# Two grouped-query attention blocks on one core: V loaded from GpSimd's DMA queue, and the remainder tiles of P of steps 24 to 125 all transposed by DMA

## The chip, the core and the metric

The kernel runs on one core of a Trainium2 chip. The core has a matrix engine (TensorE, "PE" in the profile), a vector engine (VectorE, "DVE"), a scalar engine (ScalarE, "ACT"), GpSimd ("POOL") and SyncE ("SP"), which here only issues DMAs. Sixteen DMA engines move the data. The metric is device time in microseconds, so lower is better.

## The reference

Two independent problems, A and B, of one shape; their outputs stand side by side.

```python
B, Sq, D = 16, 80, 576
Hq, Hkv, Sk, Dh = 32, 16, 512, 128           # two query heads for each K/V head
q = (x @ wq).reshape(B, Sq, Hq, Dh).transpose(0, 2, 1, 3)
k = jnp.repeat(k_cache, 2, axis=1)           # k_cache, v_cache: [16, 16, 512, 128]
v = jnp.repeat(v_cache, 2, axis=1)
scores = jnp.einsum("bhqd,bhkd->bhqk", q, k) * (Dh ** -0.5)
p = softmax(scores, axis=-1)
o = jnp.einsum("bhqk,bhkd->bhqd", p, v)
out = o.transpose(0, 2, 1, 3).reshape(B, Sq, Hq * Dh) @ wo     # [16, 80, 576]
```

All inputs and outputs are bf16.

## The kernel before, in words

**Steps.** The work is cut into 128 batch steps U. A step is one batch entry and four K/V heads, which is eight query heads, in one of the two problems. Steps 0 to 63 belong to A, 64 to 127 to B. For each step the kernel loads K (512 KB) with one transposing DMA from SyncE's queue (`ldk`, line 612) into one of five `kT` buffers, and V (512 KB) with one plain DMA from SyncE's queue (`ldv`, line 616) into one of four `v_sb` buffers.

**Five tiles of scores.** One K/V head serves two query heads of 80 rows, which makes 160 rows, and a tile has 128. So a step has four full tiles (k = 1 to 4, one for each K/V head) and one remainder tile (k = 0), which gathers the 32 rows left over from each of the four heads. TensorE computes the scores of the full tiles at line 658 (`qk`) and those of the remainder tiles at line 644 (`qkr`). For every tile VectorE takes the row maximum (line 667), ScalarE the exponential with the row sum (line 671), VectorE the reciprocal of the sums (line 677, `rcp`) and GpSimd multiplies P by it (line 680, `nrm`).

**Transposing P.** The product with V needs P with the keys on the partitions. A tile of P is 128x512, so four 128x128 transposes. The usual way is on TensorE, against an identity matrix, into PSUM (line 686, `tr`), and a copy by VectorE into `pT` (line 694 for full tiles, line 692 for the remainder tile; the operation is called `ptev`). For some steps the remainder tile goes another way: one transposing DMA from SyncE's queue writes the same place in `pT` (line 698, `rtr`). Before the change these are the odd steps from 24 to 125 except 50 to 61, 45 steps in all. In such a step the reciprocal is taken in two parts, for tile 0 alone and for tiles 1 to 4 (`RG[1]`), so there is one more reciprocal. `pT` has three buffers. The product with V is line 731 (`pv`), its result is cast into `oT` by ScalarE (line 747).

**The rest.** The projections `x @ wq` (line 540, `qp`) and `o @ wo` (line 781, `op`) are spread between the steps. Their weights come over SyncE's queue too (only problem A's first piece of wq comes from ScalarE's), and so does the output (line 815).

**Order.** Nothing is ordered at run time. A planner (`_Sched.arrange`) simulates the engines and the DMA with durations and costs that are written in the source, picks at each moment the ready operation with the lowest key on each engine, and so writes the order of each engine's instructions; waits on semaphores are put in where data cross engines. Each engine runs its list strictly in order. The planner's numbers for the operations at hand: `nrm` 0.674 us on GpSimd, `ldk` 3.4 us of SyncE, `ldv` 0.45 us of SyncE, `rtr` 1.2 us of SyncE; as DMA cost `KC` for K, `VC` for V and `RDC` (0.78) for `rtr`.

Of the kernel before, what the change touches and what calls it, by code (L numbers as in the profile page):

```python
# [19 lines left out]
NS = 16  # L20
QL0 = 15.0
QL1 = 10.0
KC = 2.95
VK = 8.0
KK = 8.0
DLAT = 1.6
XC = 0.4
QL2 = 10.0
VC = 1.65
WQC = 3.2  # L30
NQ = 3
NWS = 4
# [4 lines left out]
NWC = 4  # L37
BANKS = dict(S=(0, 1, 2, 6), T=(3, 4), O=(5, 7), M=(7, 5), M0=(7, 5, 6, 3, 4), M1=(7, 6), ML=(7, 5, 6, 0, 1))
NML = 12
XDMA = True  # L40
RG = (((0, 1, 2, 3, 4),), ((0,), (1, 2, 3, 4)))
RDMA = (24, 126)
RPER = (1, 3)
RSKIP = ((50, 62),)
XK = (15.0, 15.0)
WQK = 4.0
WQKB = 4.0
# [11 lines left out]
XLD = ((-100.0, -60.0), (-25.0, -24.9))  # L59
XH = -2.0  # L60
WQ1 = -16.8
OPX = ((12.0, 1.8), (18.5, 1.45), (18.5, 1.45), (18.5, 1.45))
LP0 = 18.5
LPS = 1.15
# [29 lines left out]
class _Sched:  # L94
# [40 lines left out]
    def arrange(self):  # L135
# [32 lines left out]
        free = dict((e, 0.9) for e in by_eng)  # L168
        mode = 0
        bank_free = dict((b, 0.0) for b in range(8))  # L170
        dma_free = 1.4
        left = len(ops)
        hold = dict(pe=0.05, dve=0.02, act=0.02, pool=0.0, sp=0.0)

# [30 lines left out]
        while left:  # L205
            best = None
            for e in free:
                cand = []
                for n in by_eng[e]:
                    if at[n] < len(streams[n]):  # L210
                        o = streams[n][at[n]]
                        r = ready(o, free[e])
                        if r is not None:
                            cand.append((r, o))
                if cand:
                    st = max(free[e], min(c[0] for c in cand))
                    if best is None or st < best[0]:
                        best = (st, e, cand)
            assert best is not None, [(streams[n][at[n]].name, [d.name for d in streams[n][at[n]].pre if d.done is None],
                                       len(streams[n][at[n]].alloc)) for n in streams if at[n] < len(streams[n])]  # L220
            now, e, cand = best
            k_, s_, r, o = min(((o.pri, o.seq, r, o) for r, o in cand if r <= now + hold[e]), key=lambda x: x[:2])
            st = max(now, r)
            o.eng = e
            dur = o.dur[e] if isinstance(o.dur, dict) else o.dur
            if e == "pe":
                if o.mode and mode == 0 or o.mode != mode:
                    st = max(st, now + 0.1)
                mode = o.mode
            if o.alloc:  # L230
                for vb, (_, b) in zip(o.alloc, pick(o.alloc, max(r, now))):
                    vb.phys = b
                    bank_free[b] = None
            o.start = st
            free[e] = st + dur
            if o.dsem is not None:
                d0 = max(st + 0.5, dma_free)
                dma_free = d0 + o.cost
                o.done = dma_free + DLAT
            else:  # L240
                o.done = st + dur + o.lat
            for res, ver in o.reads:
                if isinstance(res, _VB):
                    res.left -= 1
                    if res.left == 0:
                        bank_free[res.phys] = o.done
            at[o.stream] += 1
            left -= 1
# [75 lines left out]
def bass_concat_heads__gqa_block_cached__gqa_block_cached__near_ridge_kernel(  # L324
# [27 lines left out]
    with ExitStack() as es:  # L352
# [29 lines left out]
        S = _Sched()  # L382
# [112 lines left out]
        for goct in range(NG):  # L495
# [7 lines left out]
            for pi, (c0, c1) in enumerate(pieces):  # L503
                t_ld = 5.0 * (u0 - lead[goct]) - (WQKB if goct == NG // 2 else WQK)
                if goct < 2:
                    t_ld = (-90.0, WQ1)[goct] + (10.0, 0.02)[goct] * pi
                fr = (c1 - c0) / 1024.0
                dsem = "d_wqs" if goct == 0 and pi == 0 else "d_wqt" if goct == 1 and pi == 0 else "d_wq%d" % wsl
                eng = "act" if goct == 0 else "sp"
                strm = "wqa" if goct == 0 else "wq"  # L510

                def em_ldwa(e, wq_ap=wq_ap, q=q, wsl=wsl, c0=c0, c1=c1):
                    src = wq_ap[0:512, q * 1024 + c0:q * 1024 + c1]
                    return e.dma_start(wq_sb[:, wsl, 0:4, c0:c1], src.rearrange("(c p) n -> p c n", p=128))

                def em_ldwb(e, wq_ap=wq_ap, q=q, wsl=wsl, c0=c0, c1=c1):
                    return e.dma_start(wq_sb[64:128, wsl, 4, c0:c1],
                                       wq_ap[512:576, q * 1024 + c0:q * 1024 + c1])
# [84 lines left out]
        for U in range(NSU):  # L603
# [8 lines left out]
                return e.dma_start_transpose(kT[:, ks, :, :], src)  # L612

            def em_ldv(e, vc_ap=vc_ap, b=b, q=q, vs=vs):
                src = vc_ap[b, 4 * q:4 * q + 4, :, :].rearrange("g (p j) d -> p g (j d)", j=4)
                return e.dma_start(v_sb[:, vs, :, :], src)

            S.add("sp", 5.0 * gfirst[U] + 0.5 * (U - gfirst[U]) - LA - KK, em_ldk, writes=[R(("kT", ks), U)],
                  dsem="d_k%d" % ks, name="ldk%d" % U, stream="K", dur=3.4, cost=KC)
            S.add("sp", 5.0 * U - VK, em_ldv, writes=[R(("V", vs), U)],  # L620
                  dsem="d_v%d" % vs, name="ldv%d" % U, stream="V", dur=0.45, cost=VC)

            vo = None
            rdma = RDMA[0] <= U < RDMA[1] and U % 4 in RPER and not any(a_ <= U < b_ for a_, b_ in RSKIP)
            for k in range(5):
                T = 5 * U + k
                Q = Qof[(U, k)]
# [128 lines left out]
        for prob in range(2):  # L756
            for hh in range(NPAIR):
                for half in range(NPP):
                    for n in range(NB_):
# [47 lines left out]
                        else:  # L807
# [4 lines left out]
                            def em_st(e, rb=rb, c3=c3, prob=prob, slot=slot):  # L812
# [4 lines left out]
                            S.add("dve", xe, em_eb, reads=[R(vb, 0), R(("acc", rb, c3), (prob, hh - 1))],  # L817
                                  writes=[R(("osb", slot), (prob, half, n))], name="oeb%d.%d.%d" % (prob, half, n),
                                  stream="oeb", dur=0.38, ahead=OVO)
                            S.add("sp", xe + 0.3, em_st, reads=[R(("osb", slot), (prob, half, n))],  # L820
                                  dsem="d_out%d" % slot, name="st%d.%d.%d" % (prob, half, n), stream="st",
                                  dur=0.45, cost=0.3)

# [5 lines left out]
        def run_engine(e, name):  # L829
            for op in ops:  # L830
                if op.eng != name:
                    continue
                for ck, v in op.waits:
                    e.wait_ge(sem_of(ck), v)
                inst = op.emit(e, name) if len(op.engs) > 1 else op.emit(e)
                if op.signals:
                    if op.dsem is not None:
                        inst.then_inc(sems[op.dsem], 16)
                    else:
                        inst.then_inc(sems["e_" + name], 1)  # L840
            if name == "sp":
                for i in range(NOSB):
                    n = "d_out%d" % i
                    tot = S.totals.get(("d", n), 0)
                    if tot:
                        e.wait_ge(sems[n], tot)
# [48 lines left out]
```

## Time and profile before

| | us |
|---|---|
| median of 3 runs | 780.52 (779.81 to 781.06) |
| the profiled execution | 780.9 |
| its span, from first to last instruction | 779.2 |
| TensorE busy | 772.0 (99%), granted clock 1.00 |
| VectorE busy | 678.6 (87%) |
| ScalarE busy | 611.6 (78%) |
| GpSimd busy | 432.4 (55%) |
| moved by DMA | 166.44 MB, mean 214 GB/s |

The span is what the trace covers; 1.7 us of the execution's own time lie around it. A busy time of TensorE counts modelled ends of pipelined matmuls, so the share is read together with the time between the starts of instructions. An instruction that issues a DMA counts as no engine's busy time; SyncE's own instructions are seen in the timeline as "SPq".

### The profile page before, as it was taken

The page shows a single profiled execution, that of the slowest core. Times are in us where ns is not written, and L with a number is a line of the kernel's source. Part 1 is how long each engine was busy: PE and PEld are TensorE (multiplying, and loading weights), DVE is VectorE, ACT ScalarE, POOL GpSimd, SP SyncE. Part 2 cuts the span into 40 slices and gives each one's busy share as a digit, 9 for nine tenths or more (in the row PEclk, how much of TensorE's full clock was granted, in tenths as well). Part 3 has the DMA queues.
Part 4 walks back from the last instruction along what each step waited for, and adds up shares of the span by engine and source line. Part 5 has one row for each costly group of instructions (what it writes and reads, how often), then busy time and mean ns, then how long its engine had stood idle before and what let it go on. Part 6 is the DMA issues. An engine that isn't in the chain of part 4 may idle for free.

```text
span 779.2 us, 21256 instructions
## 1 busy us (share of the span) xinstructions
PE 772.0 (99%) x8078; PEld 567.5 (73%) x8078; DVE 678.6 (87%) x1558; ACT 611.6 (78%) x1736; POOL 432.4 (55%) x647
## 2 busy tenths in 40 slices
PE   9999999999999999999999999999999999999998
PEld 5576677777777777767777777777777777777786
DVE  4999988888888899888898899988888888989982
ACT  1878988888888888867787777978888887887860
POOL 1555755565655656555655655655655655664660
PEclk9999999999999999999999999999999999999999
DMA  9999999988899999999999999999999978999951
GB/s 249 226 259 240 249 222 247 203 188 197 205 200 213 204 237 247 251 213 227 211 229 214 177 214 244 258 218 237 221 230 202 200 177 196 257 220 210 187 134 32
DMA packets 386564, 166.44 MB, mean 214 GB/s; under 512 B 300576, under 2 KB 383008, under 8 KB 386464
## 3 DMA queue, kind: packets, MB, share of 16 engines
q1 hardware_dynamic: 385248, 163.91, 95.7%
q8 instruction: 65, 1.06, 0.6%
q10 hardware_dynamic: 1216, 1.18, 0.5%
q14 instruction: 35, 0.29, 0.1%
HBM read 87.46 MB, written 2.95 MB: 116 GB/s over the span
## 4 chain that ended last, share of the span: by engine, by line
PE 91%; DVE 7%; DMA 1%; ACT 0%; POOL 0%; issue 0%; SPq 0%
PE ps L540 20%; PE ps L781 20%; PE ps L731 17%; PE ps L686 15%; PE ps L658 13%; DVE negmax L667 4%; PE ps L644 4%; DVE pT L694 2%; DVE qT L552 1%; DMA kT<-in_A_k_cache_dram 1%; PE ps L409 0%; PE ps L464 0%; DVE pT L692 0%; ACT p_sb L671 0%; PE ps L424 0%; POOL p_sb L680 0%
## 5 line engine op out<-in xcount | busy, mean ns | idle before, releaser
L680 POOL TENSOR_SCALAR p_sb<-p_sb,rinv 128x512 bf16<-128x512 bf16 x640 | 430.0, 692 | 325.5 <-DVE rinv L677 325.1
L671 ACT ACTIVATE p_sb<-ps,negmax 128x512 bf16<-128x512 f32 x640 | 441.3, 693 | 84.0 <-DVE negmax L667 77.1
L667 DVE TENSOR_REDUCE negmax<-ps 128x1 f32<-128x512 f32 x640 | 427.8, 679 | 9.6 <-PE ps L658 5.1
L686 PE MATMUL ps<-ident,p_sb 128*128 128x128 bf16 x2380 | 229.7, 219 | 1.1 <-POOL p_sb L680 0.5
L694 DVE COPY pT<-ps 128x512 bf16<-128x512 bf16 x512 | 209.9, 413 | 16.4 <-PE ps L686 14.2
L731 PE MATMUL ps<-pT,v_sb 128*128 128x160 bf16 x2048 | 222.6, 233 | 0.1
L540 PE MATMUL ps<-xT,wq_sb 128*128 128x480 bf16 (+1 forms) x1280 | 213.2, 300 | 0.1
L731 PEld LDWEIGHTS ps<-pT,v_sb 128*128 128x128 bf16 x2048 | 158.4, 98 | 54.3 <-ACT oT L747 5.9
L686 PEld LDWEIGHTS ps<-ident,p_sb 128*128 128x128 bf16 x2380 | 168.7, 98 | 35.7 <-DVE pT L694 6.5
L658 PE MATMUL ps<-kT,qT 128*128 128x512 bf16 x512 | 189.0, 379 | 0.6 <-ACT p_sb L671 0.6
L781 PE MATMUL ps<-wo_sb,oT 128*128 128x288 bf16 x1280 | 171.5, 286 | 0.0
L540 PEld LDWEIGHTS ps<-xT,wq_sb 128*128 128x128 bf16 x1280 | 106.9, 98 | 61.4 <-ACT oT L747 2.6
L781 PEld LDWEIGHTS ps<-wo_sb,oT 128*128 128x128 bf16 x1280 | 122.8, 98 | 34.8 <-ACT qT L551 1.3
L747 ACT CAST oT<-ps 128x320 bf16<-128x320 f32 x256 | 108.7, 425 | 37.0 <-PE ps L731 36.6
L671 ACT ACTIVATION_READ_ACCUMULATOR p_sb<-ps,negmax 128x1 f32 x640 | 130.1, 203 | 0.0
L551 ACT ACTIVATE qT<-ps 128x160 bf16<-128x160 f32 (+1 forms) x159 | 63.2, 398 | 25.9 <-PE ps L540 24.9
L552 DVE TENSOR_SCALAR qT<-ps 128x480 bf16<-128x480 f32 (+1 forms) x97 | 54.7, 564 | 22.2 <-PE ps L540 21.1
L658 PEld LDWEIGHTS ps<-kT,qT 128*128 128x128 bf16 x512 | 49.2, 98 | 6.3 <-ACT p_sb L671 3.1
L809 DVE TENSOR_TENSOR osb<-ps,acc 128x288 bf16<-128x288 f32 x40 | 18.2, 456 | 27.6 <-PE ps L781 27.4
L644 PE MATMUL ps<-kT,qT 128*32 128x512 bf16 x512 | 39.6, 384 | 1.1 <-DMA kT<-in_A_k_cache_dram 0.9
L677 DVE RECIPROCAL rinv<-rowsum 128x1 f32<-128x1 f32 (+1 forms) x173 | 29.6, 171 | 11.1 <-ACT p_sb L671 11.1
L692 DVE COPY pT<-ps 128x512 bf16<-128x512 bf16 x83 | 34.5, 416 | 4.9 <-PE ps L686 4.7
(19 smaller groups left out, 47.0 us busy)
## 6 DMA issues: line engine op xcount, KB each, us to landing
v_sb<-in_A_v_cache_dram SPq DMA_DIRECT2D x64, 512.0 KB, 4.6
v_sb<-in_B_v_cache_dram SPq DMA_DIRECT2D x64, 512.0 KB, 4.6
wo_sb<-in_A_wo_dram SPq DMA_DIRECT2D x8, 576.0 KB, 7.6
wo_sb<-in_B_wo_dram SPq DMA_DIRECT2D x8, 576.0 KB, 7.4
wq_sb<-in_B_wq_dram SPq DMA_DIRECT2D x4, 1024.0 KB, 6.7
out_dram<-osb SPq DMA_DIRECT2D x40, 72.0 KB, 2.3
wq_sb<-in_A_wq_dram SPq DMA_DIRECT2D x2, 1024.0 KB, 7.4
wq_sb<-in_A_wq_dram ACTq DMA_DIRECT2D x2, 512.0 KB, 6.9
```

Source lines behind the costliest of these rows:

```text
L540: last = e.matmul(ps[:, vb.phys, 0:n1 - n0], lhsT=wq_sb[:, wsl, ck, i * 128:(i + 1) * 128], rhs=xT[:, half, ck, n0:n1], start=(ck == 0), s ...
L551: return e.activation(dst, src, AF.Identity, scale=SCALE)
L644: last = e.matmul(ps[32 * g4:32 * g4 + 32, vb_.phys, :], lhsT=qT[:, qsl_, bl_, g4 * 160 + 128:g4 * 160 + 160], rhs=kT[:, ks_, :, g4 * 128: ...
L658: return e.matmul(ps[:, vb.phys, :], lhsT=qT[:, qsl, bl, gl * 160:gl * 160 + 128], rhs=kT[:, ks, :, gl * 128:(gl + 1) * 128], start=True, ...
L667: return e.tensor_reduce(negmax[:, si:si + 1], ps[:, vb.phys, :], axis=AX.X, op=AluOpType.max, negate=True)
L671: return e.activation(p_sb[:, psl, :], ps[:, vb.phys, :], AF.Exp, bias=negmax[:, si:si + 1], scale=1.0, accum_out=rowsum[:, ss, k:k + 1])
L680: return e.tensor_scalar(p_sb[:, psl, :], p_sb[:, psl, :], rinv[:, ss, k:k + 1], 1.0, op0=AluOpType.mult, op1=AluOpType.mult)
L686: last = e.transpose(psb[:, vt.phys, j * 128:(j + 1) * 128], p_sb[:, psl, j * 128:(j + 1) * 128], ident[:])
L694: return e.tensor_copy(pT[:, pts, :, 0:4, gl * 32:gl * 32 + 32], psb[:, vt.phys, 0:512].rearrange("p (j h c) -> p j h c", j=4, h=4))
L731: last = e.matmul(ps[:, vo.phys, off:off + 160], lhsT=v_sb[:, vs, gl, j * 128:(j + 1) * 128], rhs=pT[:, pts, j, :, gl * 32:gl * 32 + 32], ...
L747: return e.copy(dst, src)
L781: last = e.matmul(ps[:, vb.phys, 0:DC], lhsT=oT[:, hi, rb * 128:(rb + 1) * 128], rhs=wo_sb[:, wi, c3 * DC:(c3 + 1) * DC], start=(hi == 0), ...
```

## The change

V is issued from GpSimd's instruction list instead of SyncE's, one DMA for each step as before, with a planned duration of 1.0 us on GpSimd (`VENG`, `VDUR`, `VN`). The remainder tile of every step from 24 to 125 is transposed by DMA (`RSEL`): 102 steps instead of 45. The planner now keeps one DMA clock for each issuing queue instead of one for all, with a cost of 2.6 for K and 1.8 for V, and writes a new order for all engines with these numbers. The other names (`STENG`, `XSH`, `WQ1B`, `VN`) keep their old meaning at these values.

```diff
-KC = 2.95
+KC = 2.6
-VC = 1.65
+VC = 1.8
...
+VENG = "pool"
+VDUR = 1.0
+VN = 1
+STENG = "sp"
...
-RDMA = (24, 126)
-RPER = (1, 3)
-RSKIP = ((50, 62),)
+RSEL = ((24, 126, (0, 1, 2, 3)),)
...
-        dma_free = 1.4
+        dma_free = {}
...
-                d0 = max(st + 0.5, dma_free)
-                dma_free = d0 + o.cost
-                o.done = dma_free + DLAT
+                d0 = max(st + 0.5, dma_free.get(e, 1.4))
+                dma_free[e] = d0 + o.cost
+                o.done = d0 + o.cost + DLAT
...
-                src = vc_ap[b, 4 * q:4 * q + 4, :, :].rearrange("g (p j) d -> p g (j d)", j=4)
-                return e.dma_start(v_sb[:, vs, :, :], src)
+                src = vc_ap[b:b + VN, 4 * q:4 * q + 4, :, :].rearrange("b g (p j) d -> p b g (j d)", j=4)
+                return e.dma_start(v_sb[:, vs:vs + VN, :, :], src)
...
-            S.add("sp", 5.0 * U - VK, em_ldv, writes=[R(("V", vs), U)],
-                  dsem="d_v%d" % vs, name="ldv%d" % U, stream="V", dur=0.45, cost=VC)
+            if U % VN == 0:
+                S.add(VENG, 5.0 * U - VK, em_ldv, writes=[R(("V", vs + i_), U + i_) for i_ in range(VN)],
+                      dsem="d_v%d" % vs, name="ldv%d" % U, stream="V", dur=VDUR, cost=VN * VC)
...
-            rdma = RDMA[0] <= U < RDMA[1] and U % 4 in RPER and not any(a_ <= U < b_ for a_, b_ in RSKIP)
+            rdma = any(a_ <= U < b_ and U % 4 in m_ for a_, b_, m_ in RSEL)
```

More of the change, by code (lines that the diff above doesn't have):

```diff
@@ L39 @@
 NML = 12
+VENG = "pool"
+VDUR = 1.0
+VN = 1
+STENG = "sp"
+XSH = 0.0
 XDMA = True
 RG = (((0, 1, 2, 3, 4),), ((0,), (1, 2, 3, 4)))
-RDMA = (24, 126)
-RPER = (1, 3)
-RSKIP = ((50, 62),)
+RSEL = ((24, 126, (0, 1, 2, 3)),)
 XK = (15.0, 15.0)
@@ L61 @@
 WQ1 = -16.8
+WQ1B = 0.02
 OPX = ((12.0, 1.8), (18.5, 1.45), (18.5, 1.45), (18.5, 1.45))
@@ L505, in bass_concat_heads__gqa_block_cached__gqa_block_cached__near_ridge_kernel @@
                 if goct < 2:
-                    t_ld = (-90.0, WQ1)[goct] + (10.0, 0.02)[goct] * pi
+                    t_ld = (-90.0, WQ1)[goct] + (10.0, WQ1B)[goct] * pi
                 fr = (c1 - c0) / 1024.0
@@ L819, in bass_concat_heads__gqa_block_cached__gqa_block_cached__near_ridge_kernel @@
                                   stream="oeb", dur=0.38, ahead=OVO)
-                            S.add("sp", xe + 0.3, em_st, reads=[R(("osb", slot), (prob, half, n))],
+                            S.add(STENG, xe + 0.3, em_st, reads=[R(("osb", slot), (prob, half, n))],
                                   dsem="d_out%d" % slot, name="st%d.%d.%d" % (prob, half, n), stream="st",
@@ L840, in run_engine @@
                         inst.then_inc(sems["e_" + name], 1)
-            if name == "sp":
+            if name == STENG:
                 for i in range(NOSB):
```

## The prediction

> **What bounds the kernel now.** I read the engine shares and the chain first, then the groups of L686, L692 and L680.
>
> ```profile
> PE 772.0 (99%) x8078; PEld 567.5 (73%) x8078; DVE 678.6 (87%) x1558; ACT 611.6 (78%) x1736; POOL 432.4 (55%) x647
> ...
> PE 91%; DVE 7%; DMA 1%; ACT 0%; POOL 0%; issue 0%; SPq 0%
> ...
> L680 POOL TENSOR_SCALAR p_sb<-p_sb,rinv 128x512 bf16<-128x512 bf16 x640 | 430.0, 692 | 325.5 <-DVE rinv L677 325.1
> ...
> L686 PE MATMUL ps<-ident,p_sb 128*128 128x128 bf16 x2380 | 229.7, 219 | 1.1 <-POOL p_sb L680 0.5
> ...
> L677 DVE RECIPROCAL rinv<-rowsum 128x1 f32<-128x1 f32 (+1 forms) x173 | 29.6, 171 | 11.1 <-ACT p_sb L671 11.1
> L692 DVE COPY pT<-ps 128x512 bf16<-128x512 bf16 x83 | 34.5, 416 | 4.9 <-PE ps L686 4.7
> ```
>
> TensorE is the path. Its idle time on DMA is about 1 us, on everything else a few us. So a matmul taken away shortens the run, if nothing else is late. The 219 ns of L686 is not the price of a transpose, because matmuls are pipelined; that is read from starts, in the timeline of TensorE:
>
> ```profile
> 305.73 0.39 PE L686 MATMUL ps<-ident,p_sb 128*128 128x128 bf16 x4
> 305.95 0.38 PE L658 MATMUL ps<-kT,qT 128*128 128x512 bf16 x1
> ```
>
> Four transposes hold TensorE for 0.22 us (56 ns each between starts over the whole trace).
>
> Then what is nearly late. SyncE's queue, in the timeline and by stretches (PE, PEld, DVE, ACT, POOL busy; clock; DMA share; GB/s):
>
> ```profile
> 58.39 0.58 SPq L616 DMA_DIRECT2D v_sb<-in_A_v_cache_dram  x1
> 59.02 3.67 SPq L612 DMA_TRANSPOSE kT<-in_A_k_cache_dram  x1
> 62.73 0.58 SPq L616 DMA_DIRECT2D v_sb<-in_A_v_cache_dram  x1
> 63.35 3.64 SPq L612 DMA_TRANSPOSE kT<-in_A_k_cache_dram  x1
> ...
> 7.00:9.00 2.00, 1.81 (x28) 1.60 (x27) 1.15 (x4) 0.19 (x1) 0.00 (x0) 1.00 1.07 374
> 58.00:80.00 22.00, 21.54 (x233) 14.81 (x232) 21.23 (x49) 18.78 (x55) 13.35 (x20) 1.00 1.04 240
> ...
> 300.00:345.00 45.00, 44.04 (x477) 32.61 (x475) 39.86 (x92) 35.98 (x104) 24.96 (x38) 1.00 1.05 247
> ...
> 480.00:540.00 60.00, 60.00 (x641) 44.17 (x634) 54.52 (x128) 50.70 (x146) 36.87 (x55) 1.00 1.03 237
> ```
>
> SyncE issues back to back. The table of waits puts some 480 us of L612 down to TensorE, but the semaphore events say otherwise: the awaited count had nearly always come before SyncE reached the instruction, and up to the last V load (landed at 749.7 us) true waits sum to about 50 us. The 3.7 us of a K issue is the queue pushing back. So the one queue runs at its own limit, near 240 GB/s in these stretches, and the second limit lies just behind TensorE. Landing to first reader shows it: K and V come about 10 us early in the median, but under 2.5 us in the median from 300 to 345 us and `rtr` 1.5 us from 480 to 540 us.
>
> Why only 240? By packets in 58 to 64 us: K alone moves at 290 GB/s (1.8 us for 512 KB), V alone at 365 (1.44 us), together 3.25 us; but a pair takes 4.35. At each turn from K to V about 1 us passes at 40 to 100 GB/s. Where two queues have work, at 7 to 9 us (SyncE's x, ScalarE's wq), it is 374 GB/s without such holes. These two are plain loads; a transposing queue beside a plain one is hardly seen.
>
> **The change part by part.** *Transposes off TensorE.* 102 steps instead of 45, so 57 tiles: 57 x 0.224 = 12.8 us off the path. The other rows of TensorE stay.
>
> *VectorE.* 57 copies of 416 ns go (23.7 us), 57 reciprocals of 171 ns come (9.7): 14 us less, off the path; 664.6 of some 768 us is again 87%.
>
> *57 more `rtr` on SyncE.* 1.21 us of issue each by the row of L698 (45 instances, 1.19 to 1.43), about 1.25 with the gap: 71 us. V's 128 issues of 0.58 us (0.62 with the gap, 79 us) leave SyncE. By issue time the queue is even: the sum of SyncE after is K 493 us, `rtr` 102 x 1.25 = 128, weights, output and x 56 and gaps, some 690 against the 740 available. So K's issue need not become shorter. Behind an `rtr` that waits for its tile stand the K loads, which are 10 us early in the median.
>
> *DMA volume.* 57 x 131 KB = 7.5 MB more: 173.9 MB. Until a last load at about 740 us that is 235 GB/s; the one queue's limit was 240. With V on a queue of its own the turns from K to V can be filled. Bounds: between nothing gained and the whole hole, 4.35 - 3.25 = 1.1 us for each step. Needed is little: 57 `rtr` at 1.25 to 1.4 us (issue, or issue and a hole) would move the last landing from 750 to 821 to 830 us if nothing is gained, V's 1.1 us would take 141 us back. Break-even for a last landing at 740 is (826 - 740) / 128 = 0.67 us for each V load. I take 0.9 to 1.1, nearest to the row at 7 to 9 us, where both queues fed the engines and no hole is left.
>
> Here a rule speaks against the change. The Trainium skill, "DMA: Bandwidth & Descriptors", section "Issuing engines are not separate DMA queues", says that issuing from several engines saves only the sequencer's issue time, since all run on the same 16 DMA engines. By that rule alone the saving would be V's issue and not the hole; the third rival has that case, worked out from rows.
>
> *128 V issues on GpSimd.* The trace has no DMA issued there. Bounds: 0.58 us (SyncE's V issue) and 3.85 (mean of SyncE's K issue, the same bytes in 2048 packets). Nearest is `rtr` on SyncE with 512 packets, as many as a V load: 1.2 us. The diff plans 1.0, and the planner's other durations are close to the trace (`nrm` 0.674 for 0.692, `rtr` 1.2 for 1.21, V on SyncE 0.45 for 0.58). I take 1.0 to 1.2: 432 + 128 x 1.1 = 573 us, 75% of the span. A step is 5.82 us now (mean from `pv` to `pv`) and 5.82 - 57 x 0.224 / 102 = 5.70 after; five `nrm` at 0.673 us between starts are 3.37, so GpSimd has 2.33 us free in each step. Behind a V issue stand the `nrm` of the next tiles, and the TensorE transposes wait for these: from `nrm` to transpose there are 3.5 us in the median, 1.4 at the tenth percentile, which covers an issue of 1.2. V's buffer is free 15.7 to 21 us before its next reader, so the issue seldom waits.
>
> *The start.* GpSimd's first list ends at 3.1 us and V0 to V3 need no free buffer, so 2 MB go out before 8 us, beside x and wq (before, V0 was issued at 18.4). x's second part landed at 7.29 us and TensorE waited for it; with three queues sharing from about 4 us on it comes 1 to 2 us later. Bounds: a loss of 2 MB at 374 GB/s, 5.6 us; a gain of the 4.8 us that TensorE lost from 20 to 100 us above its usual rate, since V is then already there. I take 1.5 us lost.
>
> *Sum.* 780.9 - 12.8 + 1.5 = 769.6 for the profiled execution, 0.4 less against the median of 780.52: **769.2**.
>
> **The rivals.** *First, slower: K and V get in each other's way.* Both queues share the 16 DMA engines, and a K transpose appears to stand until the last engine has done with V: from 349 to 351 us the rate was 132 GB/s while one engine finished V packets. If V's packets lie between K's all the time, the holes stay or grow. If the queues save only 0.4 us for each step, the last landing is 826 - 51 = 775 us; the 29 us that now follow it bring 804, and the range of savings from 0.3 to 0.55 us gives 785 to 817. For it: transposes beside plain loads are what the trace hardly shows; against it: 374 GB/s at 7 to 9 us, and the fact that V will be issued 15 us ahead. It decides below 0.67 us. Chance 0.16.
>
> *Second, slower: GpSimd becomes the bound.* Above 2.33 us for a V issue every step is longer by the excess: at 2.6 us, 0.27 x 124 = 33 us, some 800. For it: K's issue at 3.85 us shows that pushing can be long. Against: the plan's 1.0 and the `rtr` row. A way to it is a lock between VectorE and GpSimd; against that stands that the 640 `nrm` took 687 to 697 ns, all alike, beside a VectorE that was busy 87% of the time. The Trainium skill, "SBUF — State Buffer", "The 'DVE blocks DMA' trap (SWDGE)", says that GpSimd cannot write descriptors while VectorE runs a two-port mode; by the even `nrm` times no such mode is seen here. Chance 0.08.
>
> *Third, faster by less or not at all.* If V's move saves the 0.62 us of SyncE's issue and nothing of the hole, the last landing is 826 - 79 = 747 us and the end, 29 us later, 776: the queues just keep up, and TensorE waits some 7 us where the reserve was least, from 300 to 345 us and a little on (steps 50 to 61 had no `rtr` and get 12) and from 480 to 540. With 4 to 12 us of waits it is 774 to 782. For it: the reserve of under 2.5 us there; against it: the rate without holes at 7 to 9 us. Chance 0.10.
>
> That the 57 do not move at all cannot be: step numbers alone decide.
>
> **How the numbers follow.** The forecast's own case (764 to 774) has 0.62, gains at the start that bring it under 764 have 0.04. Faster by over 0.2% (about what a measurement here can tell from no change) is 0.62 + 0.04 + 0.05 of the third rival = 0.71; within 0.2% 0.03; slower 0.16 + 0.08 + 0.02 = 0.26. The range takes in the start's gain (763) and reaches into the slower cases up to 790, which leaves out some 0.2.
>
> **What would show it.** Right: L686 at 2152, L692 at 26, L698 at 102, TensorE still at 99%; the DMA rate in 58 to 80 us well over 240 GB/s; GpSimd's idle time before L680 down to about 190 us. Wrong: waits of L644, L658 or L731 for kT, v_sb or pT's DMA that sum to over 5 us (first rival), or long idle times of L686 for POOL's L680 (second).

## The result and the profile after

The changed kernel takes 845.74 us in the median of four runs (837.15 to 852.75), against 780.16 (779.27 to 781.06) of the kernel before in four runs beside it. It is slower, by a ratio of 1.075 (95% interval 1.071 to 1.079); the forecast was 769.2. Kernels with V on a second queue differ by a few per cent from run to run, so the ratios in this text are taken from their undisturbed runs.

In the profiled execution (837.15 us, span 835.4) the rows that answer to those of before are these, from the page and, in the second block, from the groups by line:

```profile
PE 773.9 (93%) x7850; PEld 561.9 (67%) x7850; DVE 669.0 (80%) x1571; ACT 611.6 (73%) x1723; POOL 531.2 (64%) x775
...
PE 78%; DVE 9%; issue 4%; DMA 4%; ACT 3%; SPq 2%; POOL 0%
...
L685 POOL TENSOR_SCALAR p_sb<-p_sb,rinv 128x512 bf16<-128x512 bf16 x640 | 429.5, 686 | 94.0 <-DVE rinv L682 90.3
...
L736 PE MATMUL ps<-pT,v_sb 128*128 128x160 bf16 x2048 | 225.7, 237 | 47.4 <-issue 31.3
...
L691 PE MATMUL ps<-ident,p_sb 128*128 128x128 bf16 x2152 | 209.9, 221 | 1.2 <-POOL p_sb L685 0.9
...
L620 POOL DMA_DIRECT2D v_sb<-in_A_v_cache_dram x64 | 50.6, 791 | 98.1 <-PE ps L691 68.3
...
L682 DVE RECIPROCAL rinv<-rowsum 128x1 f32<-128x1 f32 (+1 forms) x230 | 37.1, 164 | 8.8 <-ACT p_sb L676 8.6
```

```profile
L697 DVE COPY pT<-ps 128x512 bf16<-128x512 bf16 x26 | 10.8, 417 | 2.3 <-PE ps L691 2.2
```

The lines have moved by four or five (`ldk` is now 616, `ldv` 620, `qkr` 649, `nrm` 685, `tr` 691, `ptev` 697 and 699, `rtr` 703, `pv` 736). All that the change says has happened: 2152 transposes on TensorE, 26 copies of the remainder tile, 128 V loads from GpSimd at 0.79 us each. But TensorE is busy for 93% only, and its idle time stands before one line: 47.4 us before `pv`, where there was 0.1 before. The page writes 31.3 of it down to "issue", which is time with no releaser that it shows.

The stretches that the prediction named, with their columns (PE, PEld, DVE, ACT, POOL busy; clock; DMA share; GB/s):

```profile
7.00:9.00 2.00, 1.06 (x17) 0.88 (x17) 0.44 (x2) 0.00 (x0) 0.00 (x0) 1.00 1.04 358
58.00:80.00 22.00, 22.00 (x240) 15.68 (x238) 20.59 (x49) 18.89 (x56) 15.56 (x24) 1.00 0.89 196
300.00:345.00 45.00, 37.91 (x377) 27.31 (x374) 33.71 (x81) 31.43 (x90) 27.31 (x40) 0.95 1.06 229
480.00:540.00 60.00, 47.29 (x461) 33.52 (x459) 42.70 (x102) 37.72 (x108) 32.97 (x48) 0.89 1.03 218
```

The forecast wanted well over 240 GB/s in 58 to 80 us. There are 196, where 240 were. From 300 and from 480 us TensorE loses 7 and 13 us, and its granted clock is lower there too (0.95 and 0.89; 0.975 over the span).

Which wait it is, the chain shows at the largest gap, and SyncE's and GpSimd's timelines show what was in flight:

```profile
523.48 1.35 ACT p_sb L676 x4
524.83 0.20 ACT qT L555
525.03 9.08 issue
534.11 0.69 PE ps L736 x4
```

```profile
518.61 2.67 SPq L584 DMA_DIRECT2D wo_sb<-in_B_wo_dram  x3
521.39 2.06 SPq L703 DMA_TRANSPOSE pT<-p_sb  x1
523.49 10.36 SPq L616 DMA_TRANSPOSE kT<-in_B_k_cache_dram  x1
533.95 1.21 SPq L703 DMA_TRANSPOSE pT<-p_sb  x1
```

```profile
522.54 0.80 POOL L620 DMA_DIRECT2D v_sb<-in_B_v_cache_dram  x1 [1.09 <-PE ps L691]
```

The `rtr` issued at 521.39 us raised its semaphore at 534.02, 12.6 us later (the table of DMA issues gives 2.5 us as the median before). At 534.11 `pv` starts. So the 9.08 us called "issue" are a wait for `pT`. In front of this `rtr` on SyncE were three weight loads, and 1.15 us after it V came from the other queue. What the DMA engines did meanwhile:

```profile
521.00:523.50 2.50, 2.50 (x36) 1.79 (x28) 2.50 (x7) 2.50 (x9) 1.36 (x3) 1.00 1.01 327
523.50:528.00 4.50, 0.18 (x1) 0.00 (x0) 1.57 (x5) 1.52 (x5) 3.90 (x6) 0.82 1.53 305
528.00:532.00 4.00, 0.00 (x0) 0.00 (x0) 0.00 (x0) 0.00 (x0) 0.00 (x0) 0.50 0.65 65
532.00:534.50 2.50, 0.39 (x4) 0.42 (x5) 0.00 (x0) 0.00 (x0) 0.00 (x0) 0.50 1.17 202
```

For 4 us 65 GB/s are moved. By the packets in these 4 us, 17 to 19 are in flight the whole time, about one for each engine; yet in half a microsecond only 0 to 14 packets of the weights (51 ns each) and 1 to 13 of V (mostly 160 to 175 ns each) start. That is the work of one or two engines, in one of the eight halves that of four. The transposes' 256-byte packets take 18 ns each when all goes well, and here up to 162 ns in the mean of a half microsecond. So it looks as if one or two engines still work off plain loads, while the packets of the others stay in flight. From 534 us on, when the plain loads are through, the K load runs at 290 GB/s.

To count such moments, take the half-microseconds with over ten packets in flight on average in which the packets that ended amount to less than four engines' work, that is under 2 us, each packet counted at the median duration of its queue and size. They sum to 54 us in the trace of before and 100 us in that of after. Below it is called **stuck time**; it takes the span without the first 20 and last 40 us. Unbroken stretches of 2 us or more make 2 us of it before and 14 us after.

To see where TensorE lost its time, I compared the starts of its instructions with what the instruction before allowed. Such excess is 17.8 us before and 86.8 after: waits for `rtr` 48.6 (17 of them, up to 10.5), for weights 4.3, for `kT` 3.0, for x 2.6, and 21.8 of small pieces and lower clock (10.0 before); the remaining 6.5 lie in none of these groups. 86.8 - 17.8 - 12.8 for the work taken away = 56.2, and that is the difference of the spans.

### The profile page after: what moved, and what is told of

It reads as the page before. It is cut to its first block, busy times and chain, and to the rows that moved or that the text cites. A ratio compares the mean times of both kernels' runs of the same rounds, so it can differ in the third digit from the quotient of the medians.

```text
span 835.4 us, 20819 instructions
## 1 busy us (share of the span) xinstructions
PE 773.9 (93%) x7850; PEld 561.9 (67%) x7850; DVE 669.0 (80%) x1571; ACT 611.6 (73%) x1723; POOL 531.2 (64%) x775
## 3 DMA queue, kind: packets, MB, share of 16 engines
q0 software_dynamic: 18432, 67.12, 28.9%
HBM read 87.46 MB, written 2.95 MB: 108 GB/s over the span
## 4 chain that ended last, share of the span: by engine, by line
PE 78%; DVE 9%; issue 4%; DMA 4%; ACT 3%; SPq 2%; POOL 0%
PE ps L786 18%; PE ps L544 17%; PE ps L736 16%; PE ps L691 12%; PE ps L663 11%; DVE negmax L672 5%; PE ps L649 4%; ACT p_sb L676 2%; DVE pT L699 2%; SPq L616 2%; DMA pT<-p_sb 2%; DMA kT<-in_A_k_cache_dram 1%; DVE qT L556 1%; DMA wq_sb<-in_A_wq_dram 1%; ACT qT L555 0%
## 5 line engine op out<-in xcount | busy, mean ns | idle before, releaser
L736 PE MATMUL ps<-pT,v_sb 128*128 128x160 bf16 x2048 | 225.7, 237 | 47.4 <-issue 31.3
L699 DVE COPY pT<-ps 128x512 bf16<-128x512 bf16 x512 | 210.8, 414 | 43.5 <-PE ps L691 42.4
L736 PEld LDWEIGHTS ps<-pT,v_sb 128*128 128x128 bf16 x2048 | 162.4, 99 | 102.3 <-issue 39.4
L691 PE MATMUL ps<-ident,p_sb 128*128 128x128 bf16 x2152 | 209.9, 221 | 1.2 <-POOL p_sb L685 0.9
L663 PE MATMUL ps<-kT,qT 128*128 128x512 bf16 x512 | 193.1, 385 | 0.6 <-ACT p_sb L676 0.6
L691 PEld LDWEIGHTS ps<-ident,p_sb 128*128 128x128 bf16 x2152 | 155.1, 99 | 37.3 <-DVE pT L699 4.6
L620 POOL DMA_DIRECT2D v_sb<-in_A_v_cache_dram x64 | 50.6, 791 | 98.1 <-PE ps L691 68.3
L620 POOL DMA_DIRECT2D v_sb<-in_B_v_cache_dram x64 | 50.5, 788 | 90.8 <-PE ps L691 56.7
L556 DVE TENSOR_SCALAR qT<-ps 128x480 bf16<-128x480 f32 (+1 forms) x110 | 58.3, 531 | 36.3 <-PE ps L544 35.1
L555 ACT ACTIVATE qT<-ps 128x160 bf16<-128x160 f32 (+1 forms) x146 | 59.4, 408 | 35.3 <-PE ps L544 34.4
L682 DVE RECIPROCAL rinv<-rowsum 128x1 f32<-128x1 f32 (+1 forms) x230 | 37.1, 164 | 8.8 <-ACT p_sb L676 8.6
```

What stands on the lines that cost most here:

```text
L620: return e.dma_start(v_sb[:, vs:vs + VN, :, :], src)
L663: return e.matmul(ps[:, vb.phys, :], lhsT=qT[:, qsl, bl, gl * 160:gl * 160 + 128], rhs=kT[:, ks, :, gl * 128:(gl + 1) * 128], start=True, ...
L691: last = e.transpose(psb[:, vt.phys, j * 128:(j + 1) * 128], p_sb[:, psl, j * 128:(j + 1) * 128], ident[:])
L699: return e.tensor_copy(pT[:, pts, :, 0:4, gl * 32:gl * 32 + 32], psb[:, vt.phys, 0:512].rearrange("p (j h c) -> p j h c", j=4, h=4))
L736: last = e.matmul(ps[:, vo.phys, off:off + 160], lhsT=v_sb[:, vs, gl, j * 128:(j + 1) * 128], rhs=pT[:, pts, j, :, gl * 32:gl * 32 + 32], ...
```

## The experiments

The **theory** after these traces: transposing DMAs (K and `rtr`) go on only when all DMA engines keep step. Plain loads from a second queue let the engines drift apart, and then the transposes stand until the last engine has caught up. **Rivals**: 102 tiles are too many, whatever the queue; the new planned order is bad; GpSimd is slow as an issuer; the weights' loads do it. A summary first; V on SyncE means one queue for K, V, `rtr` and the weights.

| kernel | V from | tiles by DMA | us, median (range) | ratio to before (95%) | stuck us |
|---|---|---|---|---|---|
| before | SyncE | 45 | 780.16 (779.27 to 781.06) | 1 | 54 |
| after | GpSimd | 102 | 845.74 (837.15 to 852.75) | 1.075 (1.071 to 1.079) | 100 |
| v_pool_r0 | GpSimd | 0 | 835.99 (823.8 to 848.18) | 1.056 (lower run) | 64 |
| v_pool_r45 | GpSimd | 45 | 838.42 (835.77 to 842.82) | 1.075 (1.072 to 1.079) | 94 |
| v_sp_r102 | SyncE | 102 | 815.68 (813.25 to 817.17) | 1.045 (1.043 to 1.047) | 70 |
| v_act_r102 | ScalarE | 102 | 808.06 (807.7 to 808.42) | 1.036 (1.034 to 1.038) | 63 |
| v_four_r102 | four loads only | 102 | 776.53 (775.65 to 778.73) | 0.993 (0.990 to 0.995) | 43 |
| k_plain_r0 | GpSimd, K plain | 0 | 794.52 (791.54 to 797.5) | 1.017 (1.012 to 1.022) | 18 |

### One half of the change at a time

The 102 tiles alone, in the kernel before (v_sp_r102):

```diff
-RPER = (1, 3)
-RSKIP = ((50, 62),)
+RPER = (0, 1, 2, 3)
+RSKIP = ()
```

> Only the second half of the change: V stays on SyncE's queue, 102 remainder tiles by DMA. Theory (collision: while V's packets from a second queue are on the DMA engines, the transposes of K and of P crawl): without a second queue no rtr is slowed, but the one queue has 57 x 1.25 to 1.4 us more and only some 50 us of reserve, so 790 to 812 us, clearly under the change's 838. Rival 1 (57 more rtr are too many for the DMA engines, wherever V is issued): as slow as the change, 830 to 850. Rival 2 (GpSimd's V issues hold up nrm, and so rtr): gone here, 768 to 775.

V's move alone, in the changed kernel, with the 45 tiles of before (v_pool_r45) and with none (v_pool_r0):

```diff
-RSEL = ((24, 126, (0, 1, 2, 3)),)
+RSEL = ((24, 50, (1, 3)), (62, 126, (1, 3)))     # v_pool_r45
+RSEL = ()                                        # v_pool_r0
```

> Only the first half: V from GpSimd, the 45 remainder tiles of before by DMA, the change's planner numbers. Collision: rtr and K are slowed here too, but fewer rtr are there to be late: 785 to 815 us. Rival 1 (too many rtr): harmless or a little faster, 774 to 781. Rival 2 (GpSimd's V issues delay nrm): 785 to 800, with rtr waiting on nrm and not on the DMA engines.

> V from GpSimd, no remainder tile by DMA: TensorE has 45 x 0.224 = 10.1 us more than before, so 790.6 if nothing else is late. Collision: K is slowed beside V but is 10 us early, so 791 to 800, and V and K in flight together still move under 200 GB/s. Rival 1: 788 to 792 with a rate over 300 GB/s where both are in flight. Rival 2: 795 or more, with TensorE waiting for nrm.

The tiles alone cost 35 us (815.68 against 780.36). By the ratios, V's move alone costs 58 us with 45 tiles, and so do both together. With no tile by DMA it costs 43 us in the lower run (823.8, the one traced) and 68 in the other (848.18). These totals hide that every tile by DMA takes 0.224 us off TensorE. Set against the kernel before with as many tiles, the loss is 43 - 10.1 = 33 us with none in the lower run (58 in the other), 58 with 45 and 58 + 12.8 = 71 with 102; for the tiles alone it is 35 + 12.8 = 48. So V's move does harm without any `rtr`, and from 45 to 102 tiles it does more. With no `rtr` at all the waits go to K. The idle time before `qkr`, from the groups of v_pool_r0 by line:

```profile
L736 PE MATMUL ps<-pT,v_sb 128*128 128x160 bf16 x2048 | 227.1, 234 | 0.4 <-issue 0.4
...
L649 PE MATMUL ps<-kT,qT 128*32 128x512 bf16 x512 | 40.8, 395 | 22.5 <-issue 15.4 <-DMA kT<-in_A_k_cache_dram 3.7 <-ACT p_sb L676 3.4
```

So it is not `rtr` alone that is late, but K too. With the tiles alone the loss is of another kind: TensorE's waits for `rtr` are 16.3 us in 22 pieces, none over 1.4, and the transposes themselves land in 4.0 us in the median instead of 2.5. There the waits are many and short, as with a queue that has too much to do; its last V load lands at 791.1 us, 41 us later than before.

### The transposes, or V, taken away

In v_four_r102 only the first four steps load V, and all later ones use those buffers again; in k_plain_r0 and k_plain_r102 K is loaded by a plain DMA of the same bytes, not transposed.

```diff
-            if U % VN == 0:
-                S.add(VENG, 5.0 * U - VK, em_ldv, writes=[R(("V", vs + i_), U + i_) for i_ in range(VN)],
+            if U < NV:                                                # v_four_r102
+                S.add(VENG, 5.0 * U - VK, em_ldv, writes=[R(("V", vs), 0)],
...
-                return e.dma_start_transpose(kT[:, ks, :, :], src)
+                src = kc_ap[b, 4 * q:4 * q + 4, :, :].rearrange("g (p j) d -> p g (j d)", j=4)
+                return e.dma_start(kT[:, ks, :, :], src)              # k_plain_*
```

> The change with V loaded for the first four steps alone (all later steps use these four buffers, so the product with V is of the wrong V; all other work is done). Every theory of a collision with V: no wait for a remainder tile is left, 767 to 772 us, as the sum of the prediction without V's cost. Rival (102 transposes of P and 128 of K are too many by themselves): over 785.

> V from GpSimd, no remainder tile by DMA, and K loaded by a plain DMA of the same bytes (so K lies untransposed and the scores are of other numbers; all work is done). It is the 822 us kernel with the transposes taken off the DMA engines. Theory (transposes need all 16 engines in step, so one that lags behind with a second queue's V holds them all): the long waits are gone, TensorE alone bounds it, 789 to 796 us, and both queues together move over 330 GB/s. Rival (GpSimd's DMAs are slow beside any other queue): 810 or more.

> The change with K loaded by a plain DMA of the same bytes (K untransposed, scores of other numbers, all work done). P's 102 tiles and x of problem B are the only transposes left. If transposes wait for a lagging engine whatever they are, rtr lands late now and then: 775 to 790 us with waits for rtr of 5 to 20 us. If only K's long transposes suffer: 774 to 778 (768 and some 6 to 8 us lost at the start), no wait for rtr over 1 us.

Without V, the 102 tiles and K's transposes give 776.53 us, 0.7% under the kernel before; the excess before `pv` is 2.5 us. TensorE's 12.8 us less, those 2.5 us and a start that is 6.8 us later make 3.5 us less together; 5.5 were measured, against 782.02 beside it. The group of `pv` by line and the DMA issues of `rtr` in v_four_r102 (the last column of the issues is the median us to landing), and then the DMA issues of the changed kernel:

```profile
L736 PE MATMUL ps<-pT,v_sb 128*128 128x160 bf16 x2048 | 220.7, 233 | 2.5 <-DMA pT<-p_sb 2.4
```

```profile
pT<-p_sb SPq DMA_TRANSPOSE x102, 2.7
```

```profile
v_sb<-in_A_v_cache_dram POOLq DMA_DIRECT2D x64, 512.0 KB, 6.0
...
pT<-p_sb SPq DMA_TRANSPOSE x102, 4.9
wq_sb<-in_A_wq_dram ACTq DMA_DIRECT2D x2, 512.0 KB, 9.3
```

With V there but K plain and no `rtr` (k_plain_r0), 13 us are lost (794.52), and 10.1 of them are the 45 tiles that TensorE has back: the loss beside that falls from 33 us or more (v_pool_r0) to some 3. The stuck time falls to 18, though the same bytes go through the same two queues, and K and V in flight together move 307 GB/s (the changed kernel: 196). K then goes in packets of 1024 bytes and not of 256, so this run does not part transposing from small packets. The groups by line have before `qkr`:

```profile
L649 PE MATMUL ps<-kT,qT 128*32 128x512 bf16 x512 | 39.6, 384 | 4.6 <-DMA kT<-in_A_k_cache_dram 4.5
```

So it takes both, V's loads on a second queue and transposes: with V gone, or with all transposes of K and P gone, nearly all of the loss goes. (v_four_r102 takes V's bytes away too; that it is the queue and not the bytes, the runs with one queue below show.) k_plain_r102, with P's transposes and x's left, took 801.54 us (801.21 to 801.88, ratio 1.026, 1.023 to 1.029), 33 us above what TensorE's work would allow; its excess before `pv` for `rtr` is still 24.6 us, and one `rtr` took 17.3 us to land. The 775 to 790 us expected were missed: P's few transposes suffer as well, and more than was thought.

### The issuing engine

```diff
-VENG = "pool"
-VDUR = 1.0
+VENG = "act"
+VDUR = 0.58
```

> The change with V issued from ScalarE's queue instead of GpSimd's (ScalarE gets 128 x 0.58 = 74 us of issue on 611 busy). Collision of any second queue with transposes: 825 to 860, rtr landing 4 us and more after issue. If it is GpSimd's kind of DMA (packets of 4 KB) or its instruction list: under 800.

> V from ScalarE's queue with the 45 remainder tiles of before. If a second queue as such costs little (V on ScalarE with 102 was 808, against 816 on SyncE): 780 to 790. If any second queue beside the transposes is the damage: 800 or more. If the second queue is a gain: under 779.

From ScalarE the loss is 28 us with 102 tiles, half of that from GpSimd, and less than the tiles alone cost on one queue (815.68); it lies between the two ranges expected. With 45 tiles as in v_pool_r45 it was 820.41 (809.39 to 822.19, ratio 1.043, 1.036 to 1.050). That 45 are no better than 102 needs no further cause, since TensorE has 12.8 us more of its own work with 45: beside that work, the loss by the ratios is 34 us with 45 tiles and 28 + 12.8 = 41 with 102. The harm of ScalarE's queue is also of another make: its stuck time is 63 us with 102 tiles and 41 with 45, not above that of one queue (70 and 54), no stuck stretch lasts 2 us, and K or `rtr` and V in flight together move 238 GB/s with 102 tiles (transposes 89). So the stuck time accounts for what GpSimd's queue does, but not for ScalarE's loss. The idle time of v_act_r102 before `pv` is of the same kind as after the change:

```profile
L736 PE MATMUL ps<-pT,v_sb 128*128 128x160 bf16 x2048 | 223.6, 236 | 23.0 <-issue 22.5 <-DVE qT L556 0.4
```

Two differences between the two are seen: the page calls GpSimd's queue "software_dynamic" and SyncE's and ScalarE's "hardware_dynamic" (these are the changed kernel's queues, with packets, MB and share; q1 is SyncE's, q0 GpSimd's), and V goes in 4096 bytes a packet from GpSimd, in 1024 from ScalarE and SyncE.

```profile
q1 hardware_dynamic: 348672, 104.27, 72.2%
q0 software_dynamic: 18432, 67.12, 28.9%
q8 instruction: 63, 1.03, 0.6%
...
q14 instruction: 36, 0.29, 0.2%
```

To try the packets I laid V out so that each piece of 1 KB has its own place:

```diff
-            v_sb = sb("v_sb", [128, NV, 4, 512], BF16)
+            v_sb = sb("v_sb", [128, 4, NV, 512], BF16)
...
-                return e.dma_start(v_sb[:, vs:vs + VN, :, :], src)
+                return e.dma_start(v_sb[:, :, vs, :], src)
```

> The change, with v_sb laid out so that the four heads' rows of one partition are not adjacent: pieces of 1 KB in place of 4 KB, same bytes, same order of instructions. Theory (in each turn between the queues GpSimd's V passes 4 KB, ScalarE's 1 KB, so transposes get a smaller share and a lagging engine has more left to do): it comes near V on ScalarE's queue, 805 to 815 us, and transposes beside V move more than the 70 GB/s of the change. Rival (it is GpSimd's way of making DMAs, whatever the size): still 830 to 850.

The trace has the same 18,432 packets of GpSimd's queue as before, so the edit did not change what it was to change: 841.07 us (821.61 to 852.52) says nothing on it. Whether the packet size, the kind of queue or something else makes GpSimd's harm larger was not shown.

### The planner

All runs so far with V on another queue also had the new costs and a DMA clock for each queue. These two part them: the new planning with one queue, and the old planning with GpSimd.

```diff
-VENG = "pool"                                    # v_sp_cost_r45, with 45 tiles
-VDUR = 1.0
+VENG = "sp"
+VDUR = 0.45
...
-KC = 2.6                                         # v_pool_one_r45, with 45 tiles
-VC = 1.8
+KC = 2.95
+VC = 1.65
-                d0 = max(st + 0.5, dma_free.get(e, 1.4))
-                dma_free[e] = d0 + o.cost
+                d0 = max(st + 0.5, dma_free.get("a", 1.4))
+                dma_free["a"] = d0 + o.cost
```

> The changed kernel with V issued from SyncE again and 45 tiles by DMA, but with the changed planner: its costs of 2.6 and 1.8 and one DMA clock for each queue. Only the planned order can differ from the kernel before. Theory (transposes suffer from plain loads that come on a second queue): 775 to 787 us, since one queue is left. Rival (part of the loss is the new order, which believes that K and V no longer share a queue): 795 us or more, with the late steps in the same places as in the changed kernel.

> V from GpSimd and 45 tiles by DMA, planned with the costs (2.95 and 1.65) and the single DMA clock of the kernel before. Theory (the second queue itself): still 820 to 845 us, as with the new planning (838). Rival (the order): under 800 us.

784.3 us (781.16 to 787.79, ratio 1.003, 1.000 to 1.006) against 852.17 (824.18 to 870.89). The new order by itself costs 2 us or so, and with the old one V on GpSimd is still at least 42 us slower: the loss comes with the queue. v_sp_cost_r45 against v_pool_r45 (784.3 and 838.42) is the cleanest pair, with the same tiles, bytes and costs.

### What limits one queue, and how much a turn costs

The forecast rested on 1.1 us lost at each turn from K to V. If the turn costs that, V loaded in pairs, two steps' loads back to back, halves it. V comes from SyncE here, and the planner has one DMA clock, with 2.95 for K and 1.45 for a V load:

```diff
-VN = 1
+VN = 2
...
-                return e.dma_start(v_sb[:, vs:vs + VN, :, :], src)
+                e.dma_start(v_sb[:, vs, :, :], src[0]).then_inc(sems["d_v%d" % vs], 16)
+                return e.dma_start(v_sb[:, vs + 1, :, :], src[1])
```

> One queue, as before, 45 remainder tiles, but V is issued for two steps in a row (two DMAs back to back every second step), so the queue turns from K to V half as often. If a turn costs about 1 us: TensorE bounds it as before, 779 to 783 us, with true waits of SyncE up by 40 to 70 us. If the turns are free: waits of SyncE as before, and V, which comes later in pairs, costs 0 to 10 us.

> The same with 75 or so remainder tiles (three of four steps outside 50 to 61): 30 x 0.224 = 6.7 us less on TensorE than before, 30 x 1.25 to 1.4 = 38 to 42 us more on the queue, for which half the turns pay 70. If turns cost 1.1 us: 773 to 778, faster than before. If they are free: 790 to 800.

> The same with 102 remainder tiles. On one queue with single V loads 102 gave 816. If a pair saves one turn of 1.1 us in two steps, 70 us of queue time: 770 to 790 us. If turns are free: 810 to 820.

790.11 us with 45 tiles (ratio 1.012, 1.009 to 1.014), 797.77 with 74 (1.021, 1.018 to 1.025), 818.23 with 102 (1.047, 1.042 to 1.053). All three lie where they were expected if turns are free. After a pair the rate falls too, as here, with the K load issued at 125.88 (same columns as above):

```profile
124.00:128.00 4.00, 4.00 (x48) 3.11 (x46) 4.00 (x10) 3.62 (x10) 0.27 (x1) 1.00 0.96 277
128.00:129.75 1.75, 1.75 (x17) 1.31 (x15) 1.42 (x4) 1.75 (x6) 0.81 (x2) 1.00 1.28 53
129.75:132.00 2.25, 2.25 (x31) 1.79 (x32) 1.48 (x4) 1.30 (x4) 2.25 (x4) 1.00 1.10 202
```

Then a look at K with nothing beside it, which v_four_r102 allows. In 18 K loads that stand alone in its trace, the time from first to last packet is 2.62 us in the median (2.37 to 3.07), not the 1.8 that the prediction took from the steady rate. One of them, from 123.87 to 126.68 us:

```profile
123.95:125.25 1.30, 1.30 (x19) 0.84 (x17) 0.46 (x3) 1.26 (x5) 1.20 (x3) 1.00 0.95 132
125.25:126.60 1.35, 1.35 (x17) 0.71 (x10) 1.22 (x3) 0.28 (x1) 1.35 (x3) 1.00 1.14 257
```

Its first half is slow though no V is near. In the kernel before, 63 K loads with V beside them give the same median, 2.60 (1.86 to 4.05). So most of the "hole" belongs to the K load itself: of a pair's 4.35 us, 2.62 + 1.44 are K and V, and 0.29 are left for the turn, if nothing can fill K's slow half.

Fourteen tiles more, at places with some reserve, show how near to its limit the one queue is:

```diff
-... U % 4 in RPER and ...
+... (U % 4 in RPER or 24 <= U < 40 or 98 <= U < 110) and ...
```

> The kernel before with 14 remainder tiles more by DMA, only where SyncE's queue had reserve (even steps of 24 to 39 and 98 to 109; true waits of SyncE were about 24 us from 120 to 240 us and 20 us from 600 to 680). 14 x 0.224 = 3.1 us less on TensorE; 14 x 1.25 to 1.4 us more on the queue, 17.5 to 19.6 of the 44 us of waits. If TensorE and the one queue are the two limits: 776.5 to 778.5 us. If the queue has no room even there: 780 to 784.

783.46 us, ratio 1.002 (1.000 to 1.004): the 3.1 us that fourteen tiles take off TensorE are lost again, as is some 1.4 us more; one wait of 3.6 us for K at 312 us is the largest piece.

### Where the weights are loaded, and V's move in part

The long waits lie in stretches with weight loads. In w_small_r102, the changed kernel with most weight loads cut to a fraction of their columns, these bytes are missing. In v_part, planned with the old costs and one DMA clock, only the steps 24 to 41 and 96 to 113 take V from GpSimd, and there every remainder tile goes by DMA (63 in all).

```diff
+                        if ci >= NWS:
+                            src = src[:, 0:32]                        # w_small_r102: wo
+                    if goct >= 2:
+                        c1 = c0 + 64                                  # w_small_r102: wq
...
-                S.add(VENG, 5.0 * U - VK, em_ldv, ...
+                S.add("pool" if 24 <= U < 42 or 96 <= U < 114 else "sp", 5.0 * U - VK, em_ldv, ...   # v_part
```

> The change with the later loads of weights cut to a sixteenth of their columns (wo after the first four pieces, wq after the first two octets; the rest of these weights is stale, all work is done). If weights on SyncE's queue beside V on GpSimd's are what lets an engine fall far behind: the waits of 5 us and more go, 775 to 790 us. If V and K alone do it: 810 or more, with the loss spread evenly over the steps.

> V from GpSimd only for steps 24 to 41 and 96 to 113, far from the start and the weights' heavy stretches, all remainder tiles by DMA there; elsewhere V on SyncE and the odd steps as before: 63 tiles by DMA, 18 x 0.224 = 4.0 us less on TensorE. If the damage is confined to stretches with weights: 776.5 to 779. If V beside K costs everywhere: 782 to 795.

w_small_r102 took 800.5 and 826.74 us. In the profiled one (826.74) TensorE's waits for `rtr` are still 42.4 us and the stuck time is 94. Two runs this far apart settle no size; they show that the long waits don't need the weights' bytes. v_part took 777.0 to 802.89 in 12 runs, median 788.64, ratio 1.002 (0.999 to 1.006): even 36 steps of it make the time uneven, and nothing is gained.

## Why the prediction was wrong

**Transposes off TensorE, -12.8 us: nearly right.** In v_four_r102, where DMA is not in the way, steps 24 to 127 (from `pv` of step 23 to that of step 127) take 588.4 us against 598.9 before, 10.5 us less, and 2.5 us of waits for `rtr` are still in them.

**VectorE and GpSimd: right.** VectorE is busy for 669.0 us (664.6 forecast). A V issue on GpSimd is 0.79 us, below the 1.0 to 1.2 taken, and GpSimd has 304 us of idle time. The second rival did not occur. Two readings behind these paragraphs come out a little otherwise from the trace: a step of before is 5.76 us by the starts of `pv`, not 5.82, and from 300 to 345 us K and V land some 3 us ahead in the median, not under 2.5. Nothing hangs on either.

**SyncE's issue: right, and of no use.** What bounds SyncE is not its own issue time; an issue grows when the DMA engines do not take it up, to 10.36 us for the K issue above.

**The start, +1.5 us: too small.** The first `pv` starts at 36.1 us, 29.5 before: 6.6 us, above even the bound of 5.6. v_four_r102 has it too (36.3), v_sp_r102 not (30.1), and v_sp_cost_r45, with the new planning on one queue, not either (29.5). So it comes with the four V loads issued at once from the second queue; ScalarE's wq lands in 9.3 us instead of 6.9.

**The DMA volume: the step that failed.** The prediction set what V's own queue saves at 0.9 to 1.1 us a load, with a break-even at 0.67. In its own terms it came out so: with 102 tiles the last V load lands at 791.1 us from one queue (v_sp_r102) and at 805.9 from GpSimd's, so V's own queue saved nothing and cost (805.9 - 791.1) / 128 = 0.12 us a load (the planned orders of the two differ too). Three errors are in it. The first is the hole: K alone needs 2.62 us, not 1.8, so that of 1.1 us only 0.29 are a turn; the rest is K's own slow half, and that V could fill it was only supposed. The second is the sign. The step went by the row at 7 to 9 us, where two *plain* loads run at 374 GB/s; the row in which a transpose seemed to stand for a plain load, 132 GB/s at 349 to 351 us, was left to the first rival. The third worked the other way: the 57 tiles were priced by SyncE's issue, 1.25 to 1.4 us each, and moved the last landing on one queue by 41.4 us, 0.73 each, so that the break-even of 0.67 was too high; from 791.1 us it is 0.40, and 0.29 is still below it. After the change, K and V in flight together move 196 GB/s, of them 70 K's and `rtr`'s; before it was 222 and 101 (packets in the quarter microseconds up to 760 us in which both, and nothing else, were in flight). From GpSimd no rate was gained, and some was lost. The Trainium skill, "DMA: Bandwidth & Descriptors", "Issuing engines are not separate DMA queues", says that a second issuer saves the issue time alone; this case agrees that no bandwidth comes with it, and shows a loss beside transposes that the section does not speak of.

**The first rival: right in kind, too cheap.** It was priced by the mean rate: a saving of 0.3 us would give 817. The tiles alone on one queue (815.68) land there, but by luck: with nothing saved the same sum gives 821 to 830 us for the last landing and over 850 for the end. With V on GpSimd the price is not a rate alone but also single stalls: four waits of TensorE for `rtr` in the changed kernel take 4.9 to 10.5 us. An `rtr` is issued 9.4 us before the `pv` that reads it in the median, so a landing that takes 12.6 us instead of 2.5 comes through. From step 24 to 40 the changed kernel was even 1.7 us quicker than before; from step 40 to 90 it lost 47.6.

**The 102 tiles.** The prediction had the queue as just able to carry them with V gone. On one queue they cost 35 us, and v_sp_r59, where 14 more bring no gain, shows that 45 already stood near the limit.

**What stays open.** That one or two engines lag while the others' packets lie in flight is read from the packets; that transposes need the engines in step is inferred from it, and which engine lags was not tried. The traces hold one more sign of it. About a hundred times in a run a packet of 8 or 16 KB comes from the queues that the page calls "instruction" (16 KB take 1.07 us in the median of the changed kernel), on top of all other traffic. The 2 us from the start of such a packet are 22 to 25% of the time, but hold 27 of the 54 us of stuck time before, 49 of 100 after and 51 of 70 in v_sp_r102; with K plain and no `rtr` they hold 3 of 18. So part of the stuck time is not V's at all, and one queue has it too. Away from these packets 51 us are left after, 27 before and 15 in v_act_r102. No run tries these packets. Nor is it settled why V from GpSimd does twice the harm of V from ScalarE, or what ScalarE's harm is, which the stuck time does not show.

## What to carry to other kernels

Before a load is moved to a second queue, look at what the first queue carries: if it transposes by DMA, plain loads beside it can make it stand, and a rate seen with two plain loads does not count for it. The price of a lone operation is its time from first to last packet, not its bytes by the best rate in its middle, else its own slow half is booked as a hole that something else could fill. And before the losses of two kernels are compared, the work that one of them has more on the bounding engine is to be taken off. A chain of waits that says "issue" for 9 us on a matrix engine can mean an unseen releaser; look for the DMA whose landing coincides with the end of the gap.

## What the runs showed of the hardware

- A K load of 512 KB by transposing DMA takes 2.62 us in the median from first to last packet with nothing beside it; in the load shown, 132 GB/s in its first half and 257 in its second. A P tile of 128 KB takes 0.77 us alone (34 in v_four_r102, 0.767 to 0.818).
- With plain loads from a second queue, a transposing DMA of 128 KB took up to 13.6 us from issue to landing in the changed kernel and 17.3 in k_plain_r102; it was 6.4 at most before, 8.5 with 102 tiles on one queue. Half-microseconds of next to no progress are not the sign of a second queue: 22 GB/s at 530.0 us after, with 19 packets in flight, and 10 GB/s at 282.0 us before. What comes with GpSimd's queue is that they follow on each other.
- GpSimd issues a V load of 512 KB in 0.79 us, and its packets are of 4096 bytes; the same load from SyncE or ScalarE goes in packets of 1024.
- In the 2 us from the start of a packet of 8 or 16 KB of the "instruction" queues, transposes stood often: 27 of 54 us of stuck time in 25% of the time in the kernel before, 3 of 18 with K plain and no `rtr`.
- Where TensorE stood idle for some microseconds, its granted clock was lower, also just after it: 0.50 in the windows from 528 to 534.5 us above, and 0.89 over 480 to 540 us.
